# One more of nine score penalties on GpSimd, 64-column turnings, and four smaller edits, in a fused attention and mixture-of-experts kernel

## The chip, the cores and the metric

The kernel runs on one core of a Trainium2 chip. TensorE (PE in the profile), VectorE (DVE), ScalarE (ACT), GpSimd (POOL) and SyncE (SP, which issues most DMAs) each work through a list of instructions in order and wait for one another by semaphores. The metric is the device time of one execution in microseconds (us).

## The reference

```python
def _attn_ref(q, k, v):                      # 8 batches, 8 heads, 576 positions, 64 wide
    scores = scale * np.matmul(q, k.transpose(0, 1, 3, 2))
    kth = np.partition(scores, -32, axis=-1)[..., -32:-31]
    scores = np.where(scores >= kth, scores, -1000000000.0)
    attn = np.exp(scores - np.max(scores, axis=-1, keepdims=True))
    attn = attn / (np.sum(attn, axis=-1, keepdims=True) + 1e-09)
    return np.matmul(attn, v)

def _moe_ref(x, w_skip, w_gate, w1, w2):     # 4608 tokens of 512, 8 experts, 1024 hidden
    do_compute = x @ w_skip > 0
    out = x.copy()
    xc = x[do_compute]
    logits = xc @ w_gate
    e_idx = np.argmax(logits, axis=1)
    probs = softmax(logits)                  # gate_w is the chosen expert's
    y[mask] = gate_w[mask, None] * (np.maximum(xc[mask] @ w1[e], 0.0) @ w2[e])   # per expert e
    out[do_compute] = xc + y
```

Every query keeps its 32 best keys of 576. The attention's output is the input of the expert stage, in which each token that is not skipped goes through one expert.

## The kernel before

**Work.** The attention goes over 32 pairs of heads (p). `prep` (L543) turns queries and keys from rows into columns: nine 128x128 blocks per pair through TensorE (`turn`, L556, `nc.tensor.transpose` at L561), which ScalarE copies out. `gate_v` (L515) turns the values the same way, five blocks per pair (L526), and multiplies them with the gate's weights, so that the logits of the router come out of the attention as extra columns. `rows` (L607) makes the scores of nine tiles of 128 queries by 576 keys (products at L619), which ScalarE copies out as `XC`.

Each of the nine tiles then passes through `row` (L683). VectorE takes the eight largest of each of seven chunks (`chunk`, L690), giving 7 lists of 8; from these `cand` (L692) finds the 8 largest, strikes out values, finds the next 8, and so on, reading the first 4, 4, 6, 6 and 8 columns of the lists in its five steps. ScalarE marks what lies above the 24th value (L703), GpSimd multiplies scores and marks (`push_out`, L706) and fills nine more places (L710), VectorE takes the eight largest of that (`window`, L719), which gives the 32nd value. Last, the penalty: for every score below the 32nd value a large number, made on ScalarE (L716) or, for the tiles whose number stands in `PENS`, on GpSimd (L714). `units` (L726) makes the scores once more with keys on the partitions, adds the penalties through TensorE (L758) and takes the exponent on ScalarE; `heads` (L818) multiplies with the values (L850, L857), divides, stores, and adds the logit columns up over the four pairs of a batch (`logit`, L865). `route` (L366) turns the logits of a group of batches (four, three, one) into lists of tokens per expert; in `lists` one matrix per 128 tokens is made by comparing numbers (`rlo`, L470). Then TensorE runs eight experts one after another.

**What sets the order.** A planner (`Plan`) runs while the program is built. Every piece of work is a task with an engine, a duration booked by hand, and a due number, `NR*p + K[kind] + FINE[kind][j]`, that is a rank more than a time. On each engine it picks, among the tasks that are ready by the booked durations, the one due first. For TensorE it also books a drain (`DRAIN`) where a task uses the array in another form than the one ahead (`mode`), and it puts off such a task (`TURN`). The array has four forms here: whole (128x128, the turnings and the step that turns the row maxima at L676), four quarters (64x64), two halves of rows (64x128) and two halves of columns (128x64: `SUMS_`, the products with the values).

Of the kernel before, what the change touches and what calls it, by code (L numbers as in the profile page):

```python
# [31 lines left out]
        ("PE", "PE"): 0.0}  # L32
LOOK, GAIN, KEEP = 0.026, 6.352, 0.000
DRAIN, TURN = 0.11, 86667984302.89
K = dict(ld=-665.624, turn=-294.211, put=-160.163, swap=-358.812, rr=15.77, rc=-46.279, qk=159.612, copy=-5.616, chunk=65.783, step=7.819, cand=-158.488, cstep=-187.63, sign=11.403, fill=-141.096, push=-499.803, window=-3.908, pen=369.361, top=-210.962, flag=33.507, unit=192.182, exp=-160.426, f1=171.73, f5=-379.762, lg=-231.384, co=282.166, ce=19.07, rt=345.117, rd=148.173, rs=-447.813, moe=626.704, vt=155.686, vp=-186.981, vg=-320.687, lv=-220.575, lr=-19.092)

FINE = dict(turn=(-366.736, -634.098, -404.912), put=(216.077, -300.742, -867.113), swap=(-218.257, -250.229, -562.08, -210.477), qk=(292.243, -262.088, 352.101, 484.898, 27.898), copy=(-323.805, -220.221, 159.421, -177.437, -301.124), chunk=(-30.041, -33.338, 26.764, 61.63, -61.379, -58.647, -5.036, 17.049, -87.646), cand=(27.661, 17.891, -527.6, -542.288, -122.83, 111.441, -189.969, 13.881, 34.608), sign=(445.812, 187.864, 32.606, 218.714, 128.713, 121.369, 264.558, 221.619, 499.752), fill=(-41.807, -230.109, 225.875, 28.27, 57.436, 44.538, -24.072, 114.702, -175.062), push=(45.98, -387.537, 352.018, -87.688, 209.337, -109.418, -466.447, 193.169, -712.073), window=(-222.595, -593.193, 115.041, -457.851, -347.732, 74.368, 53.86, -22.538, -307.082), pen=(246.824, 432.902, -620.663, 287.683, 318.64, -529.283, 90.984, -471.764, 60.217), top=(139.995, 30.715, 317.049), unit=(-166.709, -371.885, -25.199, 329.457, 339.255, 305.622), exp=(-289.038, 344.611, -495.138, -433.771, 254.325, -446.067), f1=(58.774, -375.738, -668.119, -137.23, 71.463, -396.315, -493.07, -91.968, -571.16, 40.73, -249.58), f5=(-438.051, -218.375, -131.461, 263.169, -283.144, -338.662), lg=(416.756, 50.643), vt=(-96.056, -31.256), vp=(-489.313, 162.425), vg=(-180.822, 259.859))
RS = 1.0
FILLS = True
PENS = (2, 6)  # L40


@with_exitstack
def tile_kernel(ctx, tc, q, k, v, w_skip, w_gate, w1, w2, out):
# [5 lines left out]
    P = 128  # L50
# [248 lines left out]
    lg = cp.tile([P, B, KC, E + 1], F32, name="lg")  # L299
    nc.gpsimd.memset(lg, 0.0)  # L300
    wts = cp.tile([P, E], F32, name="wts")
    nc.gpsimd.iota(wts, pattern=[[-1, E]], base=E, channel_multiplier=0, allow_small_or_imprecise_dtypes=True)
# [54 lines left out]
    def route(bs, wk, due, bank=BT):  # L357
# [91 lines left out]
        def lists(j):  # L449
# [18 lines left out]
            for t in range(KC):  # L468
                e, dur, eng = on(t > 1)
                u.append(pl.add(e, dur, due, lambda t=t, eng=eng: eng.tensor_scalar(  # L470
                    L["lo1"][:, t], i128, lo[:, j * KC + t:j * KC + t + 1], None, op0=OP.is_equal), x))
# [27 lines left out]
    def load_v(p):  # L499
# [13 lines left out]
        VLOADED[p] = pl.add("SP", 2.5, NR * p + K["lv"], f, AVF.get(p - 2), first, lag=1.5)  # L513

    def gate_v(p):  # L515
        hp = p % (H // 2)
# [3 lines left out]
        for j, ts in enumerate((list(range(NM)), [NM])):  # L520
            h = Hold(BT, 1)

            def turn(h=h, ts=ts):
                pm = h()
                for i, t in enumerate(ts):
                    nc.tensor.transpose(pm[:, i * P:(i + 1) * P], VRAW[:, t].rearrange("p h d -> p (h d)"), identF)  # L526
            x = A("PE", 0.475 if j == 0 else 0.15, when(p, "vt", j), turn, RLOADED[p], VGATED.get(p - 1), take=h)
            VTURNED.setdefault(p, []).append(x)
            puts.append(A("ACT", 0.478 if j == 0 else 0.157, when(p, "vp", j), lambda h=h, ts=ts: nc.scalar.activation(
                VT[:, ts[0]:ts[-1] + 1], h.t[:, 0:len(ts) * P].rearrange("p (t c) -> p t c", c=P), AF.Copy), x, give=[h]))  # L530
# [17 lines left out]
    def prep(p):  # L548
# [120 lines left out]
    def top(p):  # L669

        t = TOP[p % 2]
        h = Hold(BT, 1)
        A = pl.add

        def turn():
            nc.tensor.matmul(h()[:, 0:P], t[:, 0:1].to_broadcast([P, P]), shift, start=True, stop=True)  # L676
        x = A("DVE", 0.08, when(p, "top", 0), lambda: nc.vector.tensor_reduce(t[:, 0:1], CL[p % 2][:, :, 0], axis=AX, op=OP.max),
              CAND[p], EXPD.get((p - 2, "all")), FLAGGED.get(p - 2))
        x = A("PE", 0.22, when(p, "top", 1), turn, x, take=h)
        TOPPED[p] = A("DVE", 0.2, when(p, "top", 2), lambda: nc.vector.tensor_reduce(t[:, 1:2], h.t[:, 0:P], axis=AX, op=OP.min), x, give=[h])  # L680

    def row(p, t):
# [45 lines left out]
        for r in range(5):  # L728
            x = A("DVE", (0.093, 0.152, 0.108, 0.166, 0.122)[r], W_("cand") + K["cstep"] * r, lambda r=r: cand(r), x)
            if r == 0:  # L730
                CAND[p].append(x)
# [8 lines left out]
        WINS[p].append(wx)  # L740
        PENNED[p].append(A("POOL" if t in pens_ else "ACT", 1.8 if t in pens_ else 0.672, W_("pen"), below_out, wx, TU.get(p - 2)))

# [84 lines left out]
    def heads(p):  # L827
# [10 lines left out]
        def values(a):  # L838
# [26 lines left out]
            def logit(j):  # L865
                if j == 0:
                    eng.tensor_tensor(lg[:, b, 0:NM], lg[:, b, 0:NM], xb[:, a, 0:NM, D:VW - 1], op=OP.add)
                elif j == 1:
                    eng.tensor_tensor(lg[0:REM, b, NM], lg[0:REM, b, NM], xb[0:REM, 1, NM, D:VW - 1], op=OP.add)
                elif j == 2:  # L870
                    eng.tensor_copy(lgr[0:REM], xb[REM:P, 1, NM, D:VW - 1])
                else:
                    eng.tensor_tensor(lg[0:REM, b, NM], lg[0:REM, b, NM], lgr[0:REM], op=OP.add)
            x, xs = None, []
# [16 lines left out]
            done.append(x)  # L891
            for j in range(4 if a else 1):
                x = A(on, 0.1 if end else 0.28, when(p, "lg", a), lambda j=j: logit(j), x, LGFREE[-1:])
                LGFREE.append(x)
                logits.append(x)
# [17 lines left out]
        STORES[p] = [A("SP", 0.62 + 1.24 * a, due, lambda a=a: put(a), done[a], lag=2.5) for a in range(2)]  # L913
        A("SP", 0.64, due + 12.0, copy_out, STORES[p], lag=2.5)
# [159 lines left out]
    PARTED = []  # L1074
    FETCHED = {(w, i): pl.add("SP", 0.5, NR * (NP - 9 + 4 * w + i) - K["ld"], lambda w=w, i=i: fetch(0, w, i), LOADED[0, NP - 9 + 4 * w + i], lag=6.0)
               for w in range(2) for i in range(4)}
# [421 lines left out]
```

## Time and profile before

| | |
|---|---|
| median of 3 runs | 1050.25 us (1047.14 to 1053.5) |
| profiled execution | 1051.28 us, span 1049.4 us |
| busy, share of the span | PE 95%, PEld 68%, DVE 86%, ACT 82%, POOL 67% |
| attention | from the start to about 793 us |
| experts | from about 798 us to the end |

PE counts a matrix product as busy until its modelled end, and PEld is the loading of its stationary operand. In the attention four engines are busy at once: in the stretch from 75 to 650 us PE 98.6%, ACT 99.4%, DVE 96.6%, POOL 83.7%. In the expert stage PE alone is full.

### The profile page before, as it was taken

Reading aid. Unit: us, or ns where it says so; the run is one execution under the profiler, and the core shown is the slowest. Engines: PE = TensorE matmul, PEld = TensorE weight load, DVE = VectorE, ACT = ScalarE, POOL = GpSimd, SP = SyncE. Lnnn points to the kernel's source line nnn. Section 1 sums busy time; section 2 is a strip of 40 time slices with the busy share of each in tenths; the row PEclk is TensorE's granted clock in tenths of the full one; section 3 lists DMA queues with packets and bytes.
Section 4 is the critical chain, followed back from the end, with each engine's and each line's share of the span. In section 5 each row is a group of like instructions: output and inputs, shape, how many; then the busy total and the mean of one; then the engine's idle time right before and its main releaser. Section 6 shows DMA issues by size and latency. Waiting matters only on the chain. (4 is left out here: it accounts for less than half of the span.)

```text
span 1049.4 us, 39975 instructions
## 1 busy us (share of the span) xinstructions
PE 1001.8 (95%) x14932; PEld 713.5 (68%) x14932; DVE 898.4 (86%) x4929; ACT 861.9 (82%) x1548; POOL 700.7 (67%) x1059
## 2 busy tenths in 40 slices
PE   6799999999999999999999999989988999999996
PEld 3456666666666666666666666656768899888995
DVE  5999998999999999999999999899986666675661
ACT  5899999999999999999999999989993344333540
POOL 2788887877888788888878898988981122210210
PEclk9799999999999999999999999999998999999998
DMA  4433434344444434444454544444224575554720
GB/s 110 101 74 87 98 87 97 89 98 99 106 93 98 98 87 93 97 108 93 106 128 111 125 106 108 117 96 92 55 55 127 168 241 180 166 159 156 222 71 28
DMA packets 270124, 116.15 MB, mean 111 GB/s; under 512 B 220520, under 2 KB 255336, under 8 KB 269920
## 3 DMA queue, kind: packets, MB, share of 16 engines
q1 hardware_dynamic: 265360, 103.73, 40.3%
q0 software_dynamic: 3360, 9.47, 2.7%
q8 instruction: 120, 1.97, 0.8%
q14 instruction: 84, 0.69, 0.2%
q10 hardware_dynamic: 1200, 0.30, 0.1%
HBM read 86.35 MB, written 24.53 MB: 106 GB/s over the span
## 5 line engine op out<-in xcount | busy, mean ns | idle before, releaser
L706 POOL TENSOR_TENSOR xw<-XC,r 128x576 f32<-128x576 f32 x288 | 365.4, 1282 | 89.1 <-ACT r L703 55.8
L690 DVE MAX8 cand<-XC 128x8 f32<-128x82 f32 (+1 forms) x2016 | 364.5, 229 | 10.9 <-ACT XC L647 10.2
L703 ACT ACTIVATE r<-XC,cl 128x576 bf16<-128x576 f32 x288 | 227.8, 796 | 3.3 <-DVE cl L696 3.0
L719 DVE MAX8 wn<-xw 128x8 f32<-128x585 f32 x288 | 214.3, 755 | 12.7 <-POOL xw L710 12.2
L619 PE MATMUL r<-TT 64*64 64x64 f32 (+1 forms) x1280 | 198.0, 424 | 1.2 <-ACT TT L566 0.4
L716 ACT ACTIVATE PEN<-XC,wn 128x576 bf16<-128x576 f32 x225 | 172.7, 794 | 2.4 <-DVE wn L719 2.2
L619 PE MATMUL r<-TS 64*64 64x512 f32 (+1 forms) x1024 | 156.2, 418 | 5.1 <-DMA TS<-TT 4.4
L696 DVE MAX8 cl<-cand 128x8 f32<-128x56 f32 (+2 forms) x864 | 156.4, 190 | 0.5
L767 PE MATMUL r<-TT 64*128 64x512 f32 (+1 forms) x528 | 146.9, 634 | 7.2 <-ACT XC L649 6.6
L800 ACT ACTIVATE PTM<-r,top 128x1024 f32<-128x1024 f32 x124 | 137.2, 1126 | 2.2 <-PE r L758 1.4
L647 ACT ACTIVATE XC<-r 128x1024 f32<-128x1024 f32 x128 | 132.3, 1041 | 7.0 <-PE r L619 6.7
L758 PEld LDWEIGHTS <-PEN 64*128 64x128 bf16 (+1 forms) x2880 | 70.6, 99 | 73.2 <-issue 69.5
L710 POOL TENSOR_SCALAR xw<-wo,CN 128x9 f32<-128x9 f32 x288 | 99.3, 345 | 25.8
L714 POOL TENSOR_SCALAR PEN<-XC,wn 128x576 bf16<-128x576 f32 x63 | 109.0, 1731 | 6.4 <-DVE cand L698 2.2
L850 PEld LDWEIGHTS pt<-VG,PTM 128*64 128x64 f32 x2432 | 84.6, 137 | 29.7 <-ACT r L703 8.1
L698 DVE MATCH_REPLACE8 cand<-cl,cand 128x28 f32<-128x28 f32 (+1 forms) x576 | 101.9, 179 | 0.0
L850 PE MATMUL pt<-VG,PTM 128*64 128x74 f32 x2432 | 97.0, 231 | 2.8 <-DVE xb L863 0.9
L619 PEld LDWEIGHTS r<-TT 64*64 64x64 f32 x1280 | 60.0, 134 | 45.4 <-issue 32.2
L1020 POOL DMA_INDIRECT xg<-xd,idx x21 | 23.6, 1124 | 98.8 <-DVE ot L1026 86.9
L1104 PE MATMUL ph<-xh,hi 128*128 128x224 f32 (+4 forms) x288 | 86.2, 299 | 1.4 <-DVE xl L1047 1.4
L1105 PE MATMUL ph<-xl,hi 128*128 128x224 f32 (+4 forms) x288 | 85.8, 298 | 0.2 <-DVE xl L1047 0.2
L1106 PE MATMUL ph<-xh,lo 128*128 128x224 f32 (+4 forms) x288 | 85.6, 297 | 0.0
(259 smaller groups left out, 2011.3 us busy)
## 6 DMA issues: line engine op xcount, KB each, us to landing
wb<-in_moe_w_dram SPq DMA_DIRECT2D x32, 512.0 KB, 4.1
raw<-in_moe_w_dram SPq DMA_DIRECT2D x28, 512.0 KB, 3.7
TS<-TT SPq DMA_DIRECT2D x64, 144.0 KB, 2.8
out_dram<-xd SPq DMA_DIRECT2D x32, 288.0 KB, 3.3
raw<-in_k_dram SPq DMA_DIRECT2D x64, 128.0 KB, 3.3
VG<-in_v_dram SPq DMA_DIRECT2D x64, 128.0 KB, 2.7
vraw<-in_v_dram SPq DMA_DIRECT2D x64, 128.0 KB, 2.6
xd<-xb SPq DMA_DIRECT2D x64, 128.0 KB, 2.5
```

Source lines behind the costliest of these rows:

```text
L619: nc.tensor.matmul(o[hs_(h)], q_, (ts[src, u:w] if y else tt[src, 0, u:w]), start=True, stop=True)
L647: nc.scalar.activation(xc[:, t:u + 1:u - t, 0:MAIN], h2.t.rearrange("p (y c) -> p y c", y=2), AF.Copy)
L690: nc.vector.max(C_[:, c], xc[:, CH[c]:CH[c + 1]])
L696: nc.vector.max(L[:, 4 * r:4 * r + 8], c)
L703: nc.scalar.activation(rr_, xc, AF.Sign, bias=CL[p % 2][:, t, 23:24], scale=-ODD, accum_out=CN[:, s:s + 1])
L706: nc.gpsimd.tensor_tensor(xw[:, 0:S], xc, rr_, op=OP.mult)
L714: nc.gpsimd.tensor_scalar(pen, xc, WN[p % 2][:, t, 7:8], None, op0=OP.is_lt)
L716: nc.scalar.activation(pen, xc, AF.Relu, bias=WN[p % 2][:, t, 7:8], scale=-1.0)
L719: nc.vector.max(WN[p % 2][:, t], xw)
L767: nc.tensor.matmul(rb[:, 512 * h + u:512 * h + w], tt[hs_(h), 0, REM + P * kc:REM + P * (kc + 1)], tt[hs_(h), 1, REM + u:REM + w], start=T ...
L800: nc.scalar.activation(o_.rearrange("p h c -> p (h c)"), i_, AF.Exp, bias=nb, scale=scale)
L850: nc.tensor.matmul(h.t[hs_(t % 2), VW * (t // 2):VW * (t // 2 + 1)], w, vg[:, a, kc], start=(kc == 0 and t < 2), stop=(kc == NM), skip_gro ...
```

## The change

1. Penalties on GpSimd: `PENS` becomes three tiles of nine in place of two (31 pairs; the last pair keeps one).
2. Candidates: the five steps of `cand` read the first 2, 2, 5, 5 and 8 columns of the seven lists.
3. Turnings: a new `flip` makes a 128x128 block as two ordinary products of 64 columns with the identity, side by side in the 128x64 form; it takes the place of `nc.tensor.transpose` in `prep` and `gate_v`. The turned maxima (`top`) are made in two halves too. These tasks now carry the mode `SUMS_`, and the planner books 0.5 us for four blocks and 0.16 us for one.
4. Sixteen products of the identity with itself stand ahead of the first turning.
5. Logit sums: both heads of a pair are added in one operation into `LGA`; the parts are put together once per batch.
6. Routing: four of five comparisons `rlo` go to VectorE in all groups, and the groups, a copy-out and a weight fetch have due numbers of their own.
7. All due numbers are new, and with them the order on every engine.

```diff
-LOOK, GAIN, KEEP = 0.026, 6.352, 0.000
+LOOK, GAIN, KEEP = 0.034, 41.466, 0.000
...
-PENS = (2, 6)
+PENS = (1, 4, 7)
...
+    for _ in range(16):
+        nc.tensor.matmul(RB[2][:, 0:P], identF, identF, start=True, stop=True)
...
+    LGA = cp.tile([P, 2, KC, E + 1], F32, name="lga")
...
-                e, dur, eng = on(t > 1)
+                e, dur, eng = ("DVE", 0.2, V_) if t > 0 else on(False)
...
+    def flip(o, x):
+        for u in range(2):
+            nc.tensor.matmul(o[hs_(u)], x[:, hs_(u)], identF, start=True, stop=True)
...
-                    nc.tensor.transpose(pm[:, i * P:(i + 1) * P], VRAW[:, t].rearrange("p h d -> p (h d)"), identF)
-            x = A("PE", 0.475 if j == 0 else 0.15, when(p, "vt", j), turn, RLOADED[p], VGATED.get(p - 1), take=h)
+                    flip(pm[:, i * P:(i + 1) * P], VRAW[:, t].rearrange("p h d -> p (h d)"))
+            x = A("PE", 0.5 if j == 0 else 0.16, when(p, "vt", j), turn, RLOADED[p], VGATED.get(p - 1), take=h, mode=SUMS_)
...
-                    nc.tensor.transpose(pm[:, j * P:(j + 1) * P], src.rearrange("p h d -> p (h d)"), identF)
+                    flip(pm[:, j * P:(j + 1) * P], src.rearrange("p h d -> p (h d)"))
...
-            x = pl.add("PE", (0.475 if p else 1.1) if len(g) > 1 else 0.15 if p else 0.42, when(p, "turn", j), turn(h, g), [LOADED[nm, p] for nm in nms], old, take=h)
+            x = pl.add("PE", 0.5 if len(g) > 1 else 0.16, when(p, "turn", j), turn(h, g), [LOADED[nm, p] for nm in nms], old, take=h, mode=SUMS_)
...
-            nc.tensor.matmul(h()[:, 0:P], t[:, 0:1].to_broadcast([P, P]), shift, start=True, stop=True)
+            o = h()
+            for u in range(2):
+                nc.tensor.matmul(o[hs_(u), 0:P], t[:, 0:1].to_broadcast([P, D]), shift, start=True, stop=True)
...
-            L, c = CL[p % 2][:, t], C_[:, :, 0:(4, 4, 6, 6, 8)[r]]
+            L, c = CL[p % 2][:, t], C_[:, :, 0:(2, 2, 5, 5, 8)[r]]
...
                 if j == 0:
-                    eng.tensor_tensor(lg[:, b, 0:NM], lg[:, b, 0:NM], xb[:, a, 0:NM, D:VW - 1], op=OP.add)
+                    if hp:
+                        eng.tensor_tensor(LGA, LGA, xb[:, :, :, D:VW - 1], op=OP.add)
+                    else:
+                        eng.tensor_copy(LGA, xb[:, :, :, D:VW - 1])
...
-            for j in range(4 if a else 1):
+            for j in range(0 if not a else 4 if hp == H // 2 - 1 else 1):
...
-                route(bs, wk, due + 30.0, RW if b == B - 2 else BT)
+                route(bs, wk, NR * p + K["rb" if b == B - 2 else "ra"], RW if b == B - 2 else BT)
```

On TensorE, at the start of the program, before:

```order
L561 MATMUL pt<-identF,raw_85 128x128 x4
L561 MATMUL pa<-identF,raw_86 128x128 x4
L561 MATMUL pt<-identF,rawr 128x128
L619 MATMUL r_147<-TT_101 64x512 x4
L619 MATMUL r_148<-TT_101 64x512 x2
```

The same place in the changed kernel (L142 is the new loop, L521 `flip`, L629 what was L619):

```order
L142 MATMUL r_149<-identF 128x128 x16
L521 MATMUL pt<-identF,raw_85 64x128 x8
L521 MATMUL pa<-identF,raw_86 64x128 x8
L521 MATMUL pt<-identF,rawr 64x128 x2
L629 MATMUL r_147<-TT_101 64x512 x4
```

Sixteen products stand ahead, every turned block is two rows of 64 columns, and the rest stands as it did.

On TensorE in the middle of the attention, before: the turning of a block of keys between products of scores (L619) and products with the values (L850), then a turning of values (L526) between other forms.

```order
L619 MATMUL r_148<-TT_102 64x512 x2
L619 MATMUL r_148<-TS_105 64x512 x2
L561 MATMUL pt<-identF,raw_85 128x128 x4
L850 MATMUL pa<-VG_131,PTM_122 64x74 x8
L850 MATMUL pa<-VG_131,PTM_123 64x74 x8
```

The same place in the changed kernel (L862 is what was L850):

```order
L629 MATMUL r_149<-TT_102 64x512 x2
L629 MATMUL r_149<-TS_105 64x512 x2
L521 MATMUL pt<-identF,raw_85 64x128 x8
L862 MATMUL pa<-VG_131,PTM_122 64x74 x8
L862 MATMUL pa<-VG_131,PTM_123 64x74 x8
```

Nothing has changed places here: four whole-array turnings became eight products of 64 columns, in the form of the rows that follow. Counted over the list of TensorE up to the first row of the experts, the 448 turned blocks were 448 instructions and are 896; the turned maxima were 32 and are 64; the array changes its form 595 times before and 493 times now; all other products have the same counts.

On TensorE a few rows later, before:

```order
L538 MATMUL pt<-GW,VT 64x18 x10
L619 MATMUL r_147<-TT_103 64x512 x2
L619 MATMUL r_147<-TT_103 64x64 x2
L526 MATMUL pt<-identF,vraw 128x128 x4
L526 MATMUL pa<-identF,vraw 128x128
L767 MATMUL r_149<-TT_101 128x512 x2
```

and in the changed kernel (L546 was L538, L779 was L767):

```order
L546 MATMUL pt<-GW,VT 64x18 x10
L629 MATMUL r_148<-TT_103 64x512 x2
L629 MATMUL r_148<-TT_103 64x64 x2
L521 MATMUL pt<-identF,vraw 64x128 x8
L779 MATMUL r_147<-TT_101 128x512 x2
```

The fifth block of the values (the single L526) has moved to a later place; the four others stand between two other forms as before, so that no change of form is saved here.

## Rows read from the trace of the kernel before

**Rows 1.** Windows of the attention: stretch, length, busy PE, PEld, DVE, ACT, POOL
```profile
75.00:650.00 575.00, 566.70 (x10202) 368.28 (x10202) 555.65 (x3482) 571.61 (x1046) 481.18 (x708) 1.00 0.44 100
650.00:700.00 50.00, 44.96 (x755) 28.84 (x755) 44.32 (x279) 45.55 (x83) 45.67 (x74) 0.97 0.50 121
sum 743.00, PE 723.76 PEld 476.36 DVE 710.29 ACT 728.00 POOL 625.87; mean PE 180.94 PEld 119.09 DVE 177.57 ACT 182.00 POOL 156.47
```

**Rows 2.** Waits of PE, 50 to 790 us: total, times, longest
```profile
PE r L767 <- ACT XC L649: 6.6, 6, 1.8
PE r L619 <- DMA TS<-TT: 2.1, 3, 1.3
...
PE r L619 <- DMA VG<-in_v_dram: 0.6, 1, 0.6
```

**Rows 3.** Timeline of PE: start, length, engine, line, operation, count
```profile
411.17 1.76 PE L850 MATMUL pt<-VG,PTM 128*64 128x74 f32 x48
412.86 1.19 PE L791 MATMUL r<-TT 64*64 64x512 f32 x8
413.89 0.45 PE L758 MATMUL r<-nbi,PEN 64*64 64x64 bf16 x18
414.27 1.13 PE L767 MATMUL r<-TT 64*128 64x512 f32 x4
```

**Rows 4.** Groups of instructions, whole program: turned values and turned maxima
```profile
L526 PE MATMUL pa<-identF,vraw 128*128 128x128 f32 x80 | 16.0, 301 | 0.8 <-DVE top L680 0.6
L526 PE MATMUL pt<-identF,vraw 128*128 128x128 f32 x80 | 16.0, 300 | 0.0
...
L676 PE MATMUL pa<-shift,top 128*128 128x128 f32 x38 | 9.2, 324 | 0.7 <-DVE cand L690 0.7
...
L676 PE MATMUL pt<-shift,top 128*128 128x128 f32 x26 | 6.3, 326 | 0.0
```

**Rows 5.** Timeline of ACT and PE around one turning of values
```profile
401.07 0.81 ACT L716 ACTIVATE PEN<-XC,wn 128x576 bf16<-128x576 f32 x1
...
401.74 0.80 ACT L703 ACTIVATE r<-XC,cl 128x576 bf16<-128x576 f32 x1
401.85 0.66 PE L526 MATMUL pa<-identF,vraw 128*128 128x128 f32 x4
...
402.34 0.27 PE L526 MATMUL pt<-identF,vraw 128*128 128x128 f32 x1
...
402.54 1.08 PE L619 MATMUL r<-TT 64*64 64x512 f32 x4
```

**Rows 6.** Timeline of the start: first turning, first products, first copy
```profile
5.99 1.09 PE L561 MATMUL pt<-identF,raw 128*128 128x128 f32 x4 [5.99 <-DMA raw<-in_k_dram]
...
11.24 0.23 PEld L619 LDWEIGHTS r<-TT 64*64 64x64 f32 x2 [0.62 <-issue]
...
12.09 0.23 PEld L619 LDWEIGHTS r<-TT 64*64 64x64 f32 x2 [0.62 <-issue]
12.35 1.02 ACT L647 ACTIVATE XC<-r 128x1024 f32<-128x1024 f32 x1 [3.61 <-PE r L619]
12.62 0.14 PEld L619 LDWEIGHTS r<-TT 64*64 64x64 f32 x2 [0.30 <-issue]
13.05 0.25 PEld L619 LDWEIGHTS r<-TT 64*64 64x64 f32 x6 [0.29 <-issue]
```

**Rows 7.** Groups by form, 75 to 675 us: penalties on POOL, two steps of `cand`
```profile
L714 POOL TENSOR_SCALAR PEN<-XC,wn 128x576 bf16<-128x576 f32 x51 | 88.2, 1731 | 6.1 <-DVE cand L698 2.2 <-DVE cl L696 2.2 <-DVE wn L719 0.5
...
L696 DVE MAX8 cl<-cand 128x8 f32<-128x56 f32 x227 | 45.8, 204 | 0.2
...
L696 DVE MAX8 cl<-cand 128x8 f32<-128x28 f32 x226 | 38.3, 175 | 0.1
```

**Rows 8.** Groups, whole program: the comparisons of the routing
```profile
L470 POOL TENSOR_SCALAR rlo<-i,rank 128x128 bf16<-128x128 f32 x28 | 17.8, 647 | 17.0 <-issue 16.8
...
L470 DVE TENSOR_SCALAR rlo<-i,rank 128x128 bf16<-128x128 f32 x12 | 4.5, 539 | 0.0
```

More of the change, by code (lines that the diff above doesn't have):

```diff
@@ L32 @@
         ("PE", "PE"): 0.0}
-LOOK, GAIN, KEEP = 0.026, 6.352, 0.000
-DRAIN, TURN = 0.11, 86667984302.89
-K = dict(ld=-665.624, turn=-294.211, put=-160.163, swap=-358.812, rr=15.77, rc=-46.279, qk=159.612, copy=-5.616, chunk=65.783, step=7.819, cand=-158.488, cstep=-187.63, sign=11.403, fill=-141.096, push=-499.803, window=-3.908, pen=369.361, top=-210.962, flag=33.507, unit=192.182, exp=-160.426, f1=171.73, f5=-379.762, lg=-231.384, co=282.166, ce=19.07, rt=345.117, rd=148.173, rs=-447.813, moe=626.704, vt=155.686, vp=-186.981, vg=-320.687, lv=-220.575, lr=-19.092)
@@ L37 @@
-FINE = dict(turn=(-366.736, -634.098, -404.912), put=(216.077, -300.742, -867.113), swap=(-218.257, -250.229, -562.08, -210.477), qk=(292.243, -262.088, 352.101, 484.898, 27.898), copy=(-323.805, -220.221, 159.421, -177.437, -301.124), chunk=(-30.041, -33.338, 26.764, 61.63, -61.379, -58.647, -5.036, 17.049, -87.646), cand=(27.661, 17.891, -527.6, -542.288, -122.83, 111.441, -189.969, 13.881, 34.608), sign=(445.812, 187.864, 32.606, 218.714, 128.713, 121.369, 264.558, 221.619, 499.752), fill=(-41.807, -230.109, 225.875, 28.27, 57.436, 44.538, -24.072, 114.702, -175.062), push=(45.98, -387.537, 352.018, -87.688, 209.337, -109.418, -466.447, 193.169, -712.073), window=(-222.595, -593.193, 115.041, -457.851, -347.732, 74.368, 53.86, -22.538, -307.082), pen=(246.824, 432.902, -620.663, 287.683, 318.64, -529.283, 90.984, -471.764, 60.217), top=(139.995, 30.715, 317.049), unit=(-166.709, -371.885, -25.199, 329.457, 339.255, 305.622), exp=(-289.038, 344.611, -495.138, -433.771, 254.325, -446.067), f1=(58.774, -375.738, -668.119, -137.23, 71.463, -396.315, -493.07, -91.968, -571.16, 40.73, -249.58), f5=(-438.051, -218.375, -131.461, 263.169, -283.144, -338.662), lg=(416.756, 50.643), vt=(-96.056, -31.256), vp=(-489.313, 162.425), vg=(-180.822, 259.859))
@@ new lines @@
+LOOK, GAIN, KEEP = 0.034, 41.466, 0.000
+DRAIN, TURN = 0.11, 139928188537078736.00
+K = dict(ld=-813.688, turn=-460.452, put=-427.08, swap=-419.279, rr=57.252, rc=-83.016, qk=14.387, copy=-16.231, chunk=66.078, step=9.966, cand=-420.693, cstep=-316.434, sign=-66.488, fill=-153.058, push=-837.656, window=-49.806, pen=424.938, top=-70.214, flag=200.392, unit=166.449, exp=-387.755, f1=30.58, f5=-698.543, lg=-191.186, co=49.961, ce=133.943, ra=258.679, rb=44.496, oc=5.539, fe=-117.168, moe=695.659, vt=-80.39, vp=-515.626, vg=-276.828, lv=-127.997, lr=405.278)
@@ new lines @@
+FINE = dict(turn=(-460.922, -826.077, -624.8), put=(377.775, -162.476, -801.7), swap=(-464.152, -350.699, -639.323, -40.218), qk=(297.896, -270.231, 391.868, 602.895, 230.858), copy=(-181.964, -74.557, 7.693, -105.751, -378.601), chunk=(-46.913, -54.267, 27.073, 37.991, -74.388, -115.171, 29.696, 10.153, -211.307), cand=(320.52, -22.581, -923.83, -129.139, -40.999, 53.252, -333.005, 80.084, 246.421), sign=(619.446, 142.338, 47.525, 483.7, 304.114, 200.151, 427.766, 107.562, 621.313), fill=(281.59, -390.687, 431.12, -309.641, 141.22, -143.606, -232.98, 331.976, -397.605), push=(113.816, -429.901, 547.469, -214.313, 371.683, 243.729, -553.166, 270.719, -962.086), window=(-164.778, -499.357, 94.118, -612.591, -490.957, 44.073, -26.692, -129.859, -527.662), pen=(496.09, 392.272, -611.006, 340.577, 143.091, -583.416, -153.75, -365.686, 90.753), top=(-355.821, 59.147, 161.221), unit=(-260.829, -349.09, 75.698, 217.676, 216.512, 236.556), exp=(-172.783, 482.841, -365.654, -342.228, 485.067, -676.9), f1=(258.371, -148.171, -495.938, 36.027, 68.223, -729.088, -625.392, -37.05, -731.621, 252.735, 46.301), f5=(-319.534, -281.718, -294.978, 195.978, -564.905, -401.198), lg=(670.705, -291.562), vt=(134.175, 275.912), vp=(-448.809, 566.199), vg=(-150.959, 47.099))
@@ L600, in tile_kernel @@
     XB = [wk.tile([P, 2, KC, VW - 1], F32, name=f"xb{i}") for i in range(2)]
+    for t in XB:
+        nc.gpsimd.memset(t[:, 0, NM], 0.0)
     SMS = [wk.tile([P, KC], F32, name=f"sm{i}") for i in range(4)]
@@ L675, in turn @@
         def turn():
-            nc.tensor.matmul(h()[:, 0:P], t[:, 0:1].to_broadcast([P, P]), shift, start=True, stop=True)
+            o = h()
+            for u in range(2):
+                nc.tensor.matmul(o[hs_(u), 0:P], t[:, 0:1].to_broadcast([P, D]), shift, start=True, stop=True)
         x = A("DVE", 0.08, when(p, "top", 0), lambda: nc.vector.tensor_reduce(t[:, 0:1], CL[p % 2][:, :, 0], axis=AX, op=OP.max),
               CAND[p], EXPD.get((p - 2, "all")), FLAGGED.get(p - 2))
-        x = A("PE", 0.22, when(p, "top", 1), turn, x, take=h)
+        x = A("PE", 0.22, when(p, "top", 1), turn, x, take=h, mode=SUMS_)
         TOPPED[p] = A("DVE", 0.2, when(p, "top", 2), lambda: nc.vector.tensor_reduce(t[:, 1:2], h.t[:, 0:P], axis=AX, op=OP.min), x, give=[h])
@@ L728, in row @@
         for r in range(5):
-            x = A("DVE", (0.093, 0.152, 0.108, 0.166, 0.122)[r], W_("cand") + K["cstep"] * r, lambda r=r: cand(r), x)
+            x = A("DVE", (0.078, 0.138, 0.1, 0.159, 0.122)[r], W_("cand") + K["cstep"] * r, lambda r=r: cand(r), x)
             if r == 0:
@@ L740, in row @@
         WINS[p].append(wx)
-        PENNED[p].append(A("POOL" if t in pens_ else "ACT", 1.8 if t in pens_ else 0.672, W_("pen"), below_out, wx, TU.get(p - 2)))
+        PENNED[p].append(A("POOL" if t in pens_ else "ACT", 1.76 if t in pens_ else 0.672, W_("pen"), below_out, wx, TU.get(p - 2)))
     XBFREE = {}
@@ L866, in logit @@
                 if j == 0:
-                    eng.tensor_tensor(lg[:, b, 0:NM], lg[:, b, 0:NM], xb[:, a, 0:NM, D:VW - 1], op=OP.add)
+                    if hp:
+                        eng.tensor_tensor(LGA, LGA, xb[:, :, :, D:VW - 1], op=OP.add)
+                    else:
+                        eng.tensor_copy(LGA, xb[:, :, :, D:VW - 1])
                 elif j == 1:
-                    eng.tensor_tensor(lg[0:REM, b, NM], lg[0:REM, b, NM], xb[0:REM, 1, NM, D:VW - 1], op=OP.add)
+                    eng.tensor_tensor(lg[:, b, 0:NM], LGA[:, 0, 0:NM], LGA[:, 1, 0:NM], op=OP.add)
                 elif j == 2:
-                    eng.tensor_copy(lgr[0:REM], xb[REM:P, 1, NM, D:VW - 1])
+                    eng.tensor_copy(lgr[0:REM], LGA[REM:P, 1, NM])
                 else:
-                    eng.tensor_tensor(lg[0:REM, b, NM], lg[0:REM, b, NM], lgr[0:REM], op=OP.add)
+                    eng.tensor_tensor(lg[0:REM, b, NM], LGA[0:REM, 1, NM], lgr[0:REM], op=OP.add)
             x, xs = None, []
@@ L891, in values @@
             done.append(x)
-            for j in range(4 if a else 1):
-                x = A(on, 0.1 if end else 0.28, when(p, "lg", a), lambda j=j: logit(j), x, LGFREE[-1:])
+            for j in range(0 if not a else 4 if hp == H // 2 - 1 else 1):
+                x = A(on, (0.2 if j == 0 else 0.13) if end else 0.42 if j == 0 else 0.28, when(p, "lg", j > 0), lambda j=j: logit(j), x if j else done, LGFREE[-1:])
                 LGFREE.append(x)
@@ L913, in heads @@
         STORES[p] = [A("SP", 0.62 + 1.24 * a, due, lambda a=a: put(a), done[a], lag=2.5) for a in range(2)]
-        A("SP", 0.64, due + 12.0, copy_out, STORES[p], lag=2.5)
+        A("SP", 0.64, due + K["oc"], copy_out, STORES[p], lag=2.5)
         XBFREE[p] = STORES[p] + logits
@@ L1074, in tile_kernel @@
     PARTED = []
-    FETCHED = {(w, i): pl.add("SP", 0.5, NR * (NP - 9 + 4 * w + i) - K["ld"], lambda w=w, i=i: fetch(0, w, i), LOADED[0, NP - 9 + 4 * w + i], lag=6.0)
+    FETCHED = {(w, i): pl.add("SP", 0.5, NR * (NP - 9 + 4 * w + i) - K["ld"] + K["fe"], lambda w=w, i=i: fetch(0, w, i), LOADED[0, NP - 9 + 4 * w + i], lag=6.0)
                for w in range(2) for i in range(4)}
```

## The prediction

> **What bounds the kernel now.** I read the windows first, because the share of the whole span mixes two stages. In the attention, from 75 to 650 us, ACT is busy 571.6 us of 575 and PE 566.7, DVE 555.7, POOL 481.2 [rows 1]. So two engines look full, DVE is 3.4% short of it and POOL 16%. Taking a penalty from ACT helps only as far as PE lets it, and the question of this change is whether PE is full or only looks so, since its busy time reaches to a modelled end.
>
> The second view is the waits of PE: the longest sum of any releaser is 6.6 us, in six waits [rows 2], and over 743 us of attention PE is idle 19.2 us (743 less 723.8) [rows 1]. The third is the timeline: each piece of PE's work starts before the one ahead has ended, 412.86, 413.89, 414.27 [rows 3]. These lengths come back unchanged in every pair. PE streams, and what is added to it comes out at the end unless it meets the 19.2 us.
>
> A rule speaks against this reading. The Trainium skill (Perfetto Trace Analysis, section Identifying the Most-Contended Engine) says that matmul busy time is no measure of headroom, and that the busy share of weight loading is. By that share, 368.3 of 575 us or 64% [rows 1], PE has a third to spare, ACT is the bound, and the kernel becomes faster (the second case below). The rows do not bear it out here: fp32 columns stream for longer than their weights take to load.
>
> **The turnings (PE).** A row of 512 fp32 columns takes 0.43 us at the full clock (12.62 to 13.05), so a column takes 0.84 ns and a row of 128 columns 0.107 us [rows 6]. A turning by transpose is one such row: 160 instructions of L526 are 160 rows [rows 4], and four of them take 0.49 us (401.85 to 402.34), which is 4 x 0.107 and 0.06 for the first [rows 5]. An ordinary fp32 product is two rows: the 32 turned maxima are 38 and 26 rows [rows 4]. So a block made of two halves is four rows of 128 columns. Halves of columns do run side by side: 48 rows of 74 columns need 48 x 74 x 0.84 ns = 2.98 us one by one, and take 1.69 (411.17 to 412.86) [rows 3]. Four rows, two at a time, are 0.214 us against 0.107. From below, the price of a block stays 0.107 (the planner books nearly that: 0.5 for four); from above it is 0.428, the halves one after another. I take 0.214, since L850 has the same form and the same type. 448 blocks x 0.107 = **+47.9 us** of PE.
>
> The Trainium skill (Perfetto Trace Analysis, section Transposes) says to use the transpose for this and not a standard product; TensorE: Matmul & The Clock Gate (section Terms) puts the transpose at four times the speed for fp32. By four the block costs 0.428, my upper end, and the sum below would be 96 us more; the rows show two rows for one, and no factor of four.
>
> **Changes of form (PE).** The list has 595 before and 493 now. One costs 0.06 us for the first row behind it and 0.09 on leaving (402.34 to 402.54 is 0.20, of which 0.107 is the row) [rows 5]: 0.15, so 102 x 0.15 = **-15.3 us** (0.09 each: -9). The turned maxima have as many columns as before in halves: between 0 and one row each less, 32 x 0.107; I take **-3**.
>
> **Waits of PE that go.** ACT makes 225 penalties now and 194 then. From one penalty to the next instruction ACT takes 0.67 us (401.07 to 401.74) [rows 5], so ACT loses 31 x 0.67 = 20.8 us. DVE reads 14, 14, 7 and 7 columns less per tile in four steps; 28 columns more cost 29 ns (175 to 204) [rows 7], so 42 columns are 44 ns, and 288 x 44 ns = 12.7 us. Both are beside PE, not on the path; what they give is fewer waits of PE. Of the 8.3 us idle from 75 to 650 us [rows 1], 2.7 are waits for DMAs [rows 2], which stay, and 5.6 can go. From 650 to 700 us PE is idle 5.0 us and POOL is busy 45.7 of 50 [rows 1]: there POOL makes comparisons of 0.65 us each [rows 8], four of five of which leave it. I take **-10.6 us**; at least 0, at most 16.5 (all but the DMAs).
>
> **What stays beside other work.** POOL gets 31 penalties of 1.73 us [rows 7], +53.7, and loses 20 comparisons, -12.9 [rows 8], and some of the logit sums, whose new form no row shows: at most +41 us on 625.9 of 743 [rows 1], which is 90%, so not the bound. If a long penalty stands ahead of a product that a window of DVE waits for, DVE is late first, and it has 5% of room. On DVE the 20 moved comparisons cost 0.54 us each [rows 8], +10.8, about what the candidates save; most come in four pairs, so up to 2 us a pair there, under the room that the longer period leaves. New orders of DMAs on SP: 0, since PE waits for DMAs 2.7 us in all.
>
> **The start.** The sixteen products are 32 rows of 128 columns. While rows of 512 columns stand 0.85 us apart (11.24 to 12.09, twice the later 0.43, the two levels of the clock) [rows 6], a row of 128 takes 0.21, so they last 6.8 us at most from about 1.3 us on, to 8.1; the first turning starts at 5.99 now. It is up to 2.1 us late, and twice as long, but the four steps of the first scores then take 1.7 us, not 3.4. The first copy, 12.35 now, moves by -1.5 to +2 us: I take **0**. The expert stage has the same instructions: 0.
>
> **Sum.** 47.9 - 15.3 - 3 - 10.6 = +19.0 us. The profiled execution took 1051.28 us (span 1049.4), so 1070.3; it lies 1.0 above the median of the runs, which gives **1069 us** against 1050.25.
>
> **Rivals.**
> *ACT was the bound, or the halves cost what the planner books.* Then PE falls by 18 us, ACT by 20.8 (728 to 707) and DVE by 2 (710 to 708) [rows 1]. With some 20 us of idle time on both, as DVE and PE have now, the 743 us become 728 or 729: **1036 us**. For it: ACT 99.4% busy, and fewer changes of form. Against it: PE's even spacing, and two rows per product.
> *The new order hides it.* PE's need grows by 29.6 us (all terms but the waits), ACT, DVE and POOL have room, all 19.2 us of PE's idle time go, and changes of form cost a little more than I read (0.2 us): some +5, **1054 us**. It decides where PE is left no wait at all. Against it: waits for DMAs remain.
> *PE's waits grow.* The planner books four turned blocks at 0.5 where I count 0.86, 1.2 us too little per pair, so it puts other engines' work in an order for a faster PE, and DVE's comparisons stand behind POOL's longer row. If the idle time stays and 10 us come on top: +40, **1090 us**. It decides where buffers are held longer than booked.
>
> **How the numbers follow.** About 0.5% (5 us) is what a measurement of this kernel can tell from no change. My case 0.58 (its own range 1058 to 1084, by 0 to -16.5 for the waits and -9 to -16 for the forms), ACT as the bound 0.18, hidden 0.14, growing waits 0.10. The first and the last are slower, 0.68; a fifth of the hidden one is too, 0.03, against as much of mine that may end within 0.5%. So faster 0.18, same 0.14, slower 0.68. The range takes in most of the faster case and leaves out the far end of the last: 1036 to 1084.
>
> **What would show it.** After: rows of `flip` four to a block, 0.21 us apart by block at the full clock; PE still idle under 3% in the attention while ACT falls below 97% and DVE below 95%; the end of the attention later than 793 us by some 20; the expert stage as long as before. I am wrong if four turned blocks take about 0.5 us, if PE shows waits for ACT in every pair, or if ACT stays over 99%.

## The result, and the profile after

The changed kernel takes 1061.06 us (median of 4 runs, 1056.87 to 1062.34) beside 1049.45 for the kernel before: ratio 1.010, 95% interval 1.0057 to 1.0142. It is slower, by 11.6 us, and the whole interval lies above 1. The time is inside the forecast's range and 8 us under its value. The profiled execution took 1062.34 us, span 1060.6; against the profile of before that is +11.1 us.

Windows of the changed kernel, columns as in [rows 1]: stretch, length, busy PE, PEld, DVE, ACT, POOL; then the granted clock of PE, the DMA share and GB/s.

```profile
50.00:75.00 25.00, 24.91 (x449) 17.12 (x450) 23.11 (x141) 24.01 (x46) 22.97 (x28) 1.00 0.35 78
75.00:650.00 575.00, 570.55 (x10959) 388.89 (x10956) 541.82 (x3410) 552.71 (x1001) 497.44 (x633) 1.00 0.43 98
650.00:700.00 50.00, 49.47 (x951) 34.17 (x949) 49.37 (x303) 46.95 (x84) 44.26 (x59) 1.00 0.46 112
700.00:793.00 93.00, 92.08 (x1883) 64.88 (x1879) 88.10 (x534) 88.33 (x160) 83.47 (x115) 1.00 0.35 80
sum 743.00, PE 737.01 PEld 505.06 DVE 702.40 ACT 712.00 POOL 648.14; mean PE 184.25 PEld 126.26 DVE 175.60 ACT 178.00 POOL 162.03
```

PE is now idle 6.0 us of 743 (743 less 737.0) where it was 19.2 [rows 1]; ACT fell from 99.4% to 96.1% of the long stretch and DVE from 96.6% to 94.2%. The one engine left near its limit is PE.

Waits of PE from 50 to 800 us, the longest sums (releaser: total, times, longest), to be held against [rows 2]:

```profile
PE r L779 <- ACT PTM L812: 1.6, 2, 1.3
PE r L480 <- DVE LS L483: 1.0, 1, 1.0
PE pa L862 <- ACT TT L574: 0.8, 1, 0.8
```

No transfer stands among them any more: the 2.1 us for `TS` and the 0.6 for the values are gone.

Timeline of PE, one pair's key blocks and what follows them:

```profile
404.12 1.09 PE L521 MATMUL pt<-identF,raw 128*64 128x128 f32 x16
405.04 2.23 PE L862 MATMUL pa<-VG,PTM 128*64 128x74 f32 x64
```

Four blocks are now sixteen rows, and the next piece of work starts 0.92 us after their first, where four whole transposes and the change of form behind them take about 0.59 before. The start of the program, to be held against [rows 6]:

```profile
1.36 6.67 PE L142 MATMUL r<-identF 128*128 128x128 f32 x32 [1.36 <-POOL identF masks.py:199]
7.96 1.09 PE L521 MATMUL pt<-identF,raw 128*64 128x128 f32 x16
...
12.60 1.02 ACT L657 ACTIVATE XC<-r 128x1024 f32<-128x1024 f32 x1 [1.86 <-PE r L629]
```

The first turning starts 1.97 us later and the first copy 0.25 us later. The expert stage begins at 805.60 and not at 794.78, and then takes 255.0 us where it took 254.6, so the whole difference lies in the attention.

### The profile page after: what moved, and what is told of

It reads as the page before. It is cut to its first block, busy times and chain, and to the rows that moved or that the text cites. A ratio compares the mean times of both kernels' runs of the same rounds, so it can differ in the third digit from the quotient of the medians.

```text
span 1060.6 us, 42761 instructions
## 1 busy us (share of the span) xinstructions
PE 1031.9 (97%) x16372; PEld 758.3 (72%) x16372; DVE 896.7 (85%) x4948; ACT 852.5 (80%) x1517; POOL 725.1 (68%) x969
## 4 chain that ended last, share of the span: by engine, by line
PE 87%; ACT 6%; DVE 4%; issue 1%; DMA 1%; POOL 0%; SPq 0%; POOLq 0%; DVEq 0%; ACTq 0%
PE r L629 15%; PE r L779 10%; PE pa L862 8%; PE pt L862 7%; PE pt L521 6%; PE pa L521 5%; PE ph L1120 4%; PE ph L1119 4%; PE ph L1121 4%; PE py L1142 4%; PE py L1144 4%; PE py L1143 4%; PE r L770 3%; PE r L803 3%; PE r L790 3%; ACT PEN L728 1%
## 5 line engine op out<-in xcount | busy, mean ns | idle before, releaser
L702 DVE MAX8 cand<-XC 128x8 f32<-128x82 f32 (+1 forms) x2016 | 358.6, 229 | 14.2 <-ACT XC L657 13.4
L715 ACT ACTIVATE r<-XC,cl 128x576 bf16<-128x576 f32 x288 | 223.7, 781 | 3.3 <-DVE cl L708 2.0
L629 PE MATMUL r<-TT 64*64 64x512 f32 (+1 forms) x1280 | 194.5, 419 | 3.0 <-ACT XC L657 2.3
L726 POOL TENSOR_SCALAR PEN<-XC,wn 128x576 bf16<-128x576 f32 x94 | 162.8, 1733 | 7.6 <-PE pt L869 1.4
L629 PE MATMUL r<-TS 64*64 64x512 f32 (+1 forms) x1024 | 162.0, 419 | 2.6 <-DMA TS<-TT 2.5
L708 DVE MAX8 cl<-cand 128x8 f32<-128x14 f32 (+2 forms) x864 | 151.1, 183 | 0.5
L728 ACT ACTIVATE PEN<-XC,wn 128x576 bf16<-128x576 f32 x194 | 147.6, 775 | 1.6 <-DVE wn L731 1.4
L779 PE MATMUL r<-TT 64*128 64x512 f32 (+1 forms) x528 | 144.7, 625 | 2.4 <-ACT PTM L812 1.6
L722 POOL TENSOR_SCALAR xw<-wo,CN 128x9 f32<-128x9 f32 x288 | 100.5, 349 | 26.4
L710 DVE MATCH_REPLACE8 cand<-cl,cand 128x14 f32<-128x14 f32 (+1 forms) x576 | 96.3, 170 | 0.0
L629 PEld LDWEIGHTS r<-TT 64*64 64x64 f32 x1280 | 59.4, 133 | 46.1 <-issue 30.2
L972 ACT ACTIVATE hi<-wb 128x1024 fp32r<-128x1024 f32 x32 | 33.7, 1059 | 62.7 <-PE py L1144 62.4
L1048 POOL DMA_INDIRECT out_dram<-ot,idx x21 | 21.6, 1027 | 90.1 <-DVE ot L1041 47.8
```

The lines of the kernel that those rows point to most:

```text
L629: nc.tensor.matmul(o[hs_(h)], q_, (ts[src, u:w] if y else tt[src, 0, u:w]), start=True, stop=True)
L702: nc.vector.max(C_[:, c], xc[:, CH[c]:CH[c + 1]])
L715: nc.scalar.activation(rr_, xc, AF.Sign, bias=CL[p % 2][:, t, 23:24], scale=-ODD, accum_out=CN[:, s:s + 1])
L726: nc.gpsimd.tensor_scalar(pen, xc, WN[p % 2][:, t, 7:8], None, op0=OP.is_lt)
L728: nc.scalar.activation(pen, xc, AF.Relu, bias=WN[p % 2][:, t, 7:8], scale=-1.0)
L779: nc.tensor.matmul(rb[:, 512 * h + u:512 * h + w], tt[hs_(h), 0, REM + P * kc:REM + P * (kc + 1)], tt[hs_(h), 1, REM + u:REM + w], start=T ...
```

## The experiments

Ratios are to the kernel before on the same chip; the changed kernel's is 1.010. "Whole transposes" means the changed kernel with this edit, its order left as it is:

```
     def flip(o, x):
-        for u in range(2):
-            nc.tensor.matmul(o[hs_(u)], x[:, hs_(u)], identF, start=True, stop=True)
+        nc.tensor.transpose(o, x, identF)
```

**Whole transposes.**

> The changed kernel in its own order, with each turned block again one transpose of 128x128. Theory: the same 49 us come back as in the halves of one row, but PE changes its form 582 times instead of 493, 89 x 0.10 to 0.15 = 9 to 13 us more; so 1030 to 1048 us, and above the halves of one row. Rival (a change of form costs nothing by itself): equal to the halves of one row. Rival (the new order is what costs): 1055 us or more.

1036.7 us, ratio 0.9861 (0.9836 to 0.9885): faster than both kernels, by intervals that lie apart. Undoing the halves alone gives back 24.4 us.

**Halves alone, in the kernel before** (its two `nc.tensor.transpose` of L526 and L561 replaced by `flip`, order and table kept).

> The kernel before in its own order, with each turned block as two ordinary halves: the one edit alone, neither penalties nor candidates nor comparisons moved. Theory: +49 us of PE, 80 changes of form less (595 to 515), -12 us, and a slower PE swallows 10 to 16 us of its own waits though ACT got no relief: 1068 to 1078 us. Rival (the waits of PE went because ACT, DVE and POOL were relieved): they stay here, 1083 to 1090 us. Rival (halves are hidden): 1050 us.

1076.93 us, ratio 1.0262 (1.0236 to 1.0288), as the theory had it. The halves cost 26.4 us in the old order, so the rest of the change, its order included, is a gain in either company: 1.0262 to 1.010, or 1 to 0.9861.

**Halves of one row** (shortened: in the run the two views stand written out in the call).

```
-            nc.tensor.matmul(o[hs_(u)], x[:, hs_(u)], identF, start=True, stop=True)
+            hi = lambda a: a.bitcast(BF).rearrange('p (c two) -> p c two', two=2)[:, :, 1]
+            nc.tensor.matmul(o[hs_(u)], hi(x[:, hs_(u)]), hi(identF), start=True, stop=True)
```

> The changed kernel in its own order; only the turned blocks read the upper 16 bits of each number and of the identity, as bf16, so that each half is one row of 128 columns and not two (the lower 16 bits are left out). Nothing else changes: same instructions, same shapes, same places. Theory (PE bounds, and the second row of each half is the cost): PE needs 448 x 0.109 = 49 us less than in the changed kernel, which is more than its waits allow; the attention falls until ACT (712 us busy of 743) has some 15 us left, so 1020 to 1037 us. Rival (the halves lie beside other work, or the new order is what costs the time): 1055 to 1062 us.

The total, 1283.54 us, missed every expectation. The windows of the attention and of the last stretch show why:

```profile
0.00:775.00 775.00, 730.18 (x14007) 478.55 (x14009) 741.23 (x4659) 740.04 (x1362) 678.13 (x926) 0.99 0.44 99
...
1030.00:1281.00 251.00, 73.56 (x328) 62.21 (x328) 96.28 (x514) 20.09 (x22) 4.11 (x4) 0.53 0.11 37
```

The turned values feed the gate, and with their lower bits left out the routing came out otherwise: a last stretch of 251 us runs a part of the program (L1395 to L1480) that runs in neither the kernel before nor the changed one. The attention can be read all the same. PE has the same products there, with fewer rows in the turned blocks alone, and the attention ends at 775.3 us, 30.3 before the changed kernel's; with the 255 us of the changed kernel's experts that would be an estimated 1030 us, inside the theory's range. ACT and DVE are busy some 740 of 775 us and PE 730, so PE is no longer the engine nearest its limit. Whole transposes end the attention at 780.1 us, 4.8 us later, as their expectation had it for changes of form that cost something.

**Values in halves only** (keys and queries whole), a part dose.

> The changed kernel with whole transposes for the 288 blocks of keys and queries and halves for the 160 blocks of values alone. Theory (each block in halves costs PE the same, and PE bounds from the first): 160/448 of the way from 0.9861 to 1.010, that is 0.9946, +-0.003. Rival (ACT bounds at first and hides a part dose): 0.986 to 0.990.

1047.35 us, ratio 0.9947 (0.9922 to 0.9972), where the straight line gives 0.9946. No floor hides the first blocks. The line by count is only roughly the right one: the array still changes form 583 times here (586 with whole transposes, 497 with halves throughout), so the blocks of values save hardly a change, and by the rule of the table below they put 15.3 of the 34.7 us of all halves on PE. A line by that work gives 0.9966, inside the interval too.

**Penalties back on ACT, with whole transposes and with halves.** The order is kept; row 4 of each of 31 pairs is issued to ACT:

```
-            if t in pens_:
+            if t in pens_ and t != 4:
                 nc.gpsimd.tensor_scalar(pen, xc, ...)
```

> The changed kernel in its own order with whole transposes (1036.7 us, 0.986 of before), and 31 of its 94 penalties on POOL (every row 4) issued to ACT in the place where they stand. Theory: with whole transposes ACT is near its limit again, and 31 x 0.67 = 20.8 us of ACT come out as waits of PE in part: +8 to +18, 1045 to 1055 us. Rival (the gain against before has nothing to do with ACT: it is PE's fewer changes of form and the start): 1036 to 1039 us.

> The changed kernel as it is (halves, 1.010 of before) with 31 penalties issued to ACT where they stand: the same 20.8 us of ACT that cost 0.98% with whole transposes. Theory (with the halves PE alone bounds, and ACT has some 22 us more room): half of that or less, +0 to +0.5%, 1.010 to 1.015. Rival (the two costs simply add): +0.9 to +1.1%, 1.019 to 1.021.

With whole transposes the ratio goes from 0.9861 to 0.9959 (0.9938 to 0.9979), about 1% or 10 us; with halves from 1.010 to 1.0107 (1.0064 to 1.0149), nothing that can be measured, and the rival's 1.019 to 1.021 is outside the interval. The windows from 75 to 650 us, first whole transposes as they are, then these with the penalties back, then halves with the penalties back:

```profile
75.00:650.00 575.00, 565.91 (x10314) 369.08 (x10314) 557.83 (x3537) 563.50 (x1033) 513.35 (x653) 1.00 0.45 101
```

```profile
75.00:650.00 575.00, 561.60 (x10217) 363.51 (x10219) 552.75 (x3492) 568.38 (x1045) 466.15 (x623) 1.00 0.44 101
```

```profile
75.00:650.00 575.00, 568.80 (x10885) 387.06 (x10876) 538.52 (x3391) 559.58 (x1018) 453.20 (x601) 1.00 0.43 97
```

With whole transposes PE is idle 9.1 us of 575; the penalties put ACT at 98.8% and PE's idle time at 13.4. With halves and the same load ACT stands at 97.3% and PE is idle 6.2.

**Comparisons back on POOL**, with whole transposes: first all but one in five (24 comparisons, more than the expectation's 20), then just the 20 that the change moved.

```
     e, dur, eng = ("DVE", 0.2, V_) if t > 0 else on(False)
-    u.append(pl.add(e, dur, due, lambda t=t, eng=eng: eng.tensor_scalar(
+    u.append(pl.add(e, dur, due, lambda t=t, eng=(nc.gpsimd if t > 1 else eng): eng.tensor_scalar(   # first run
+    u.append(pl.add(e, dur, due, lambda t=t, eng=on(t > 1)[2]: eng.tensor_scalar(                    # second run
```

> As the changed kernel with whole transposes (1036.7 us), some 20 of the routing's comparisons issued to POOL in the place where they stand, 0.65 us each there instead of 0.54 on DVE. Theory (the waits of PE round the routing, 5 us from 675 to 700 us in the kernel before, came from these): +3 to +6, 1039 to 1043 us. Rival (they stand beside other work): 1036 to 1038 us.

> As the changed kernel with whole transposes (0.9861 of before), and just the 20 comparisons that the change moved issued to POOL where they stand; the earlier run had also sent the last batch's to POOL, three of each five of which were on DVE before. Theory (most of that run's +0.6% was the last batch's, on which the expert stage waits): +0 to +0.3%, 0.986 to 0.989. Rival (comparisons on POOL cost PE wherever they stand): +0.5% or more, 0.991 and up.

The first gave 0.9923 (0.9904 to 0.9943), +0.6%, above what the theory gave it. Its place is in the waits of PE from 50 to 790 us:

```profile
PE r L480 <- POOL rlo L474: 4.9, 8, 1.3
```

All eight stand between 772 and 782 us. That is not the last batch, as the second expectation says, but the second group, batches 4 to 6, the last to be routed before the expert stage begins; the last batch's five comparisons come behind 807 us, inside the expert stage. The first run had undone too much: three in five of these two groups' were on DVE before (`on(late)`), and only the first group's were all on POOL. With just the 20 the ratio is 0.9895 (0.9864 to 0.9926) and the wait this:

```profile
PE r L480 <- POOL rlo L474: 2.3, 3, 1.2
```

These stand in the second group again, of whose 15 comparisons the change moved three. The time is +0.3% over 0.9861 with intervals that overlap: the sign is likely, the size open.

**Candidates and products ahead**, each undone by its own lines, with whole transposes.

> As the changed kernel with whole transposes (1036.7 us), its ranking again over 4, 4, 6, 6, 8 columns a chunk, in the same order: 288 x 44 ns = 12.7 us more of DVE. Theory (PE and ACT bound, DVE has some 3% of room): 0 to +4, 1037 to 1041 us. Rival (DVE's relief is what shortened the waits): +8 to +13, 1045 to 1050 us.

> As the changed kernel with whole transposes (1036.7 us), without the 16 products of the identity at the start. Theory: the products last from 1.4 to about 8 us, the keys land about 6 us, and in return the first scores run at the full clock: -2 to +3, no clear difference, 1034 to 1040 us. Rival (the clock they save carries the start): +4 to +6, 1041 to 1043 us.

0.9874 (0.9855 to 0.9894) and 0.9863 (0.984 to 0.9885): neither can be told from 0.9861, as forecast.

**Halves in the first three pairs only** (`flip` takes the transpose where p > 2).

> The changed kernel with whole transposes, but halves in the first three pairs, where PE waits for DVE and its granted clock is 0.50 to 0.91 between 20 and 50 us (0.93 from 40 to 50 us with halves throughout, 0.60 with whole transposes). Theory (a busier PE keeps the clock and the full period is reached earlier): -1 to -4 us, 0.982 to 0.985. Rival (DVE sets this stretch, busy 5.0 of 5 us): no difference, 0.985 to 0.988.

0.9868 (0.9825 to 0.991). From 25 to 50 us, first with whole transposes, then so:

```profile
25.00:50.00 25.00, 21.34 (x197) 12.07 (x195) 24.41 (x167) 20.27 (x43) 20.91 (x23) 0.68 0.49 104
```

```profile
25.00:50.00 25.00, 21.27 (x270) 12.44 (x272) 24.64 (x169) 21.20 (x44) 21.30 (x24) 0.93 0.52 111
```

The granted clock rises from 0.68 to 0.93 and DVE is busy 24.4 to 24.6 of these 25 us, as the rival had it. The interval of the time takes in both expectations; the traces decide: the twelfth `window` of DVE starts at 51.10 us with whole transposes and at 51.34 so, no earlier with the higher clock.

**Old turnings, rest of the change, booked as before**, so that the planner makes a new order from the changed table.

> The changed kernel with the turnings as before, transposes booked and grouped as before, everything else of the change kept; the planner makes an order of its own from the new table. Theory: PE needs about as much as before, ACT 20.8 us and DVE 2 us less, so the waits of PE fall from some 25 us towards 10: 1036 to 1048 us, faster than both if the order is no worse. Rival (the rest of the change is what costs): 1055 us or more.

1083.53 us, ratio 1.0302 (1.0279 to 1.0325), a miss by 35 us. Its instructions are those of whole transposes; only what the planner books for the turnings differs (0.475 and 0.15 for 0.5 and 0.16, and another `mode`). Waits of PE from 30 to 800 us:

```profile
PE pt L688 <- DVE LS L483: 13.2, 1, 13.2
PE pt L688 <- DVE top L689: 8.6, 1, 8.6
PE r L779 <- ACT XC L659: 7.3, 4, 2.7
```

Two single waits make 21.8 us. This says little of the edits; it says that the new table gives a good order only with the bookings that it was fitted to. All the other runs keep the order of their kernel.

## Why the prediction was right, and by how much it missed

The table is worked out from four traces: each row of PE in the attention is given the time to the next row's start. What exceeds its columns at the full clock (0.056 us at least) by more than 0.09 us, or 0.125 across a change of form, counts as wait, so slow-clock time at the start is in there too, and shorter waits stay in the work. Each entry is total (without waits), in us.

```
                       before         halves alone   changed        whole transposes
turned blocks           80.3 ( 69.4)  118.8 (113.0)  119.1 (112.7)   81.9 ( 68.9)
scores, 64x64 (L619)   214.0 (198.3)  207.4 (195.4)  201.1 (191.5)  206.0 (193.7)
values (L850, L857)    204.2 (202.5)  199.8 (197.5)  198.8 (198.1)  205.0 (204.2)
turned maxima           13.2 ( 12.6)   14.2 ( 12.8)   10.4 ( 10.3)   10.5 ( 10.5)
routing (L476)           7.3 (  2.5)    6.8 (  2.5)    2.9 (  1.9)    2.9 (  1.9)
products ahead             -              -            6.6 (  5.9)    6.4 (  5.7)
the rest               269.8 (263.4)  267.0 (262.4)  265.3 (262.4)  266.2 (263.5)
sum                    788.8 (748.7)  814.0 (783.5)  804.2 (782.9)  778.8 (748.2)
waits                   40.1           30.6           21.4           30.5
changes of form          596            516            497            586
first row at             5.99           4.34           1.36           1.36
attention ends at      794.8          818.4          805.6          780.1
```

**What bounds it.** Shown, in both directions: taking out the halves gave 24.4 us, a part dose fell on the line, and a load on ACT that costs 10 us without the halves costs nothing that can be measured with them. The Trainium skill (Perfetto Trace Analysis, section Identifying the Most-Contended Engine) judges PE's headroom by the share of weight loading, with the arithmetic done as a share of the peak beside it. By that share PE would have had 32% to spare in the changed kernel (388.9 of 575 us); these runs go against it for this kernel. That the time lies inside the range says little by itself, since 1036 to 1084 takes in faster kernels too; the terms below say more.

**The turnings.** Forecast 0.214 us a block against 0.107. One block and four take, to the next piece of work, 0.259 and 0.586 us before, and 0.269 and 0.924 after (medians of the groups). That is 0.109 and 0.218 a block: 448 x 0.109 = 48.8 us where 47.9 was forecast. The factor of four in the Trainium skill (TensorE: Matmul & The Clock Gate, section Terms) does not show here: it is two.

**Changes of form.** Forecast -15.3 at 0.15 us each. In one order, with and without halves, there are 497 and 586; PE's work without waits differs by 34.6 us (782.85 less 748.25), so 48.8 less 34.6 is 14.2 us for 89 changes, 0.16 each. The old order with and without halves gives 0.18 for 80 changes, and other limits for what counts as wait give 0.15 to 0.2, so the size is rough. The turned maxima gave 2.3 us where 3 was forecast. Together the three terms were to be +29.6; without the products ahead PE's work grew by 28.2 (782.9 less 5.9, less 748.7).

**The start.** Forecast 0. The products cost 5.9 us and the first row starts 4.6 earlier: +1.3. What the clock gives back behind them is among the waits in this table. The first copy of scores comes 0.25 us later, and without the products (whole transposes) the time is the same.

**Waits of PE that go: the term that was mis-sized.** Forecast -10.6, measured -18.7 (40.1 to 21.4). Fixed times hold different work in kernels of different length, so stretches are cut here where DVE starts the 12th, 21st, 241st and 257th of its 288 `window`s; in the kernel before that is at 51, 75, 652 and 704 us. By the rule of the table 11.1 us went from 75 to 704 us, which is about what the forecast counted; 2.4 went from 51 to 75 us, 2.5 from 704 us to the end of the attention, and 2.6 in the first 51 us. So the sum was near in its own stretch and put nothing on the others. By the windows, PE's idle time from 50 to 793 us fell by 13.2 of its 19.2 us, between the 10.6 of the main case and the 19.2 of the rival "the new order hides it". The two windows of before that the forecast left out:

```profile
50.00:75.00 25.00, 22.33 (x412) 14.91 (x414) 23.80 (x152) 24.95 (x49) 21.26 (x24) 1.00 0.35 78
...
700.00:793.00 93.00, 89.77 (x1811) 64.33 (x1809) 86.53 (x476) 85.89 (x151) 77.76 (x123) 1.00 0.27 60
```

The reasons given for the term hold only in part. The forecast had ACT's and DVE's relief take the waits from 75 to 650 us, and the comparisons that leave POOL those from 650 to 700 us. PE's idle time in these stretches, in us, worked out from the four traces:

```
stretch (times of before)   before   halves alone   changed, penalties on ACT   changed
start to 51                  14.5       12.5                  9.0                 9.1
51 to 75                      2.3        1.3                  0.0                 0.0
75 to 652                     8.3        8.4                  6.3                 4.6
652 to 704                    5.0        3.5                  1.1                 0.4
704 to the end                4.5        4.2                  2.3                 2.0
```

Halves alone move no work from one engine to another. The slower PE by itself covers nothing in the long stretch and 1.5 us of the next; the whole change but the penalties covers 2.0 and 3.9, with the penalties 3.7 and 4.6. By the rule of the table the penalties put back on ACT add 8.9 us of waits with whole transposes and 1.9 with halves. So ACT's relief is a small part of the 18.7, and that the forecast came near in its stretch is in part luck.

The waits for transfers (2.7 us) were held to stay, and they went. In the changed order, from 50 to 775 us, the traces list none with halves, 2.4 us with whole transposes and 6.4 us with halves of one row, where PE has least to do; probably a later PE finds the transfers landed.

So 28.2 + 1.3 - 18.7 = +10.8 us, the attention's, against a forecast of +19.0.

**Slips in the working.** They change no verdict. The bounds of the main case add up to 1063 to 1086 us, not 1058 to 1084, and the measured 1061 is just under them. The rival's +5 gives 1055 us, not 1054. The comparisons were priced on DVE at their mean length, 0.54 us, but they overlap: 12 of them kept DVE busy 4.5 us [rows 8] and the 32 of the changed kernel 10.8 us, so the 20 cost 6.3 us there and not 10.8.

**What stays beside other work.** The candidates were put at nothing, and no difference could be told. POOL was put under 90%, and 497.4 of 575 us is 86.5%. The relief of ACT, put under the waits, is worth 1% without halves and nothing that can be measured with them, so in the changed kernel it is spent on an engine that no longer bounds. The moved comparisons were held to cost or give little; where their place shows in PE's waits is the second group, routed right ahead of the experts, in which PE's products wait for those on POOL.

**What stays open.** Halves alone to the changed kernel is 1.6%, and the penalties are not in it. By the table it is fewer waits (9.2, of which the penalties are 1.9), an earlier first row (3.0) and smaller pieces of PE's work, less the products ahead (5.9). How much of the other waits belongs to the order, to the comparisons or to the joint sums of the logits was not taken apart; the joint sums were never undone. Which order would suit whole transposes booked at their own price was not found; the one that was tried is 1.0302.

Of the signs named, four blocks in sixteen rows, PE idle under 3%, ACT below 97%, DVE below 95% and an expert stage of the same length came; the end of the attention is 10.8 us later, not 20.

## What to carry to other kernels

Count an operation in rows before judging it by its instructions: here an fp32 product is two rows and a transpose one, so replacing 448 blocks' transposes by products doubled their stream, and the changes of form that it saved paid for about a third. A change that bundles relief for one engine with a load on another should be split by undoing one part in the changed order, because the relief was worth 10 us or nothing that could be measured, depending on which engine bounds. When work is added to the engine that bounds, price the waits that it covers stretch by stretch and over the whole stage: here the added work alone covered none in the long steady stretch and some at the start and round the routing.

## What was not expected of the hardware

The granted clock of PE between 25 and 50 us could be lifted from 0.68 to 0.93 by giving PE more rows, and the work beside it came no earlier, since DVE was busy 24.4 of 25 us there. Changes of the array's form cost PE some 0.16 us each over 89 of them (0.15 to 0.2 by the limits chosen), and part of that shows in the neighbours: the product with the values, whose instructions are the same, takes 198.1 us beside halves and 204.2 beside whole transposes.
